# The first unit's rows asked for before a slot's scatter, and their sums and splits in order of use

## The chip, the cores and the metric

One core of a Trainium2 chip runs the whole program. The metric is the device time of one execution in microseconds (us); the median of several runs is compared. TensorE (PE) multiplies matrices, VectorE (DVE) and ScalarE (ACT) work on tiles elementwise, GpSimd (POOL) copies and issues indirect transfers, SyncE (SP) issues most of the other transfers.

## What is computed

```python
attn_out = attention(q, k, v, mem_k, mem_v)     # 4 x 8 heads, 768 tokens, chunks of 32 with a local window
x = attn_out as (3072 tokens, 512)
# routed part: each token goes to one of 8 experts
for e in range(8):
    h = np.maximum(x[mask] @ w1[e], 0.0)        # 512 -> 1024
    out[mask] = gate_w[mask, None] * (h @ w2[e])  # 1024 -> 512
# dense part, on the routed part's output
h = x @ w_in                                    # 512 -> 2048
r = np.maximum(h, 0.0)
return ((r * r) @ w_out).astype(np.float32)     # 2048 -> 512
```

## The kernel before, in words

The program has three parts that run one after the other with some overlap: attention, the routed part, the dense part. Every float32 product is made of three matmuls, on a high and a low part of each operand (`split`, lines 105 and 108: ScalarE casts the high part, VectorE subtracts it from the source).

**The routed part** works through 28 slots of 128 tokens (`s`, up to `NA` = 28; a further three, `NA` to `NS`, stand under a condition at line 1662 and are run only where the number of slots in use asks for them). For each slot: the tokens' rows are gathered (`gather`, POOL), transposed and split (`xtr`), multiplied by the expert's first weights in two halves (`mm1 a`, `mm1 b`, tiles `wh1a`, `wl1a` and so on, PSUM `hps`), passed through ScalarE (`ha`, `hb`), transposed and split (`htr`, tiles `tr`, `hThb`, ...), and multiplied by the second weights (`mm2 a`, `mm2 b`, PSUM `yps`). `finish` (line 1156) scales the result on ScalarE into `ysb`, and POOL scatters it by an indirect transfer (line 1157) to `y_d` in HBM, where the rows stand in the order of the tokens. The weights' high and low tiles are made anew (`renew`, line 998) only where the next slot has another expert; SP then also loads the following expert's raw weights (`r1a` ... `r2b`, line 1015).

**The dense part** (`Ffn`) takes the rows of `y_d` in three units of 1024 tokens. `load_y(u, r)` (line 1266) asks on SP for four tiles of 128 rows, for r = 0 and r = 1; `ytr` (line 1277) transposes them into the four PSUM banks X, Y, Z and W; `ycw` is a list of twelve steps that forms seven operands from the four banks, sums and differences first (`tu`, `tv`, lines 1291 and 1306), then for each a split into `yc` and `yl` (`put`). The first product is a seven-product scheme: `product` (line 1336) is called in the order of operands 1, 6, 5, 7 and then 2, 3, 4 (`FIRST`, `SECOND`), 42 matmuls in all for one step `d`. The second product (`second`, lines 1357 to 1359, PSUM `acc`) follows one step behind.

**How the two meet.** `run` is a generator: `prep` for the first unit's rows, then eight steps `d` and `rest` for each unit. Each `yield` ends a chunk. In the slot loop `ffn_step` is called four times a slot, and in the last slots each call draws one chunk from it:

```python
            if s < NA - 3 or (s == NA - 3 and n < 2):
                return
            n = 1
            while n and pending[0] != "acc":
```

So chunks are drawn from the last call of slot 25 on. After the slot loop a loop over the remaining chunks runs the dense part and, after every second one, `conv.step()`. `conv` (`Convert`) turns w_in and w_out from 64-bit to 32-bit numbers in 64 pieces: an ACT-issued load `rw`, a ScalarE step (line 182), four VectorE operations (lines 190 to 199) and the split. The last 16 pieces, of w_out, are left for the dense part.

The engines execute their instructions in the order in which this code issues them, and tiles of one tag share a buffer: an instruction waits until the buffer's earlier users are done. `y_d` is one tensor for all scatters: a read waits for the scatters issued before it, and a scatter for the reads issued before it.

Of the kernel before, what the change touches and what calls it, by code (L numbers as in the profile page):

```python
# [21 lines left out]
def kernel(  # L22
# [31 lines left out]
    NA = NT + E // 2  # L54
# [48 lines left out]
    def split(hi, lo, src, eng=nc.vector, cp=None):  # L103
        if cp is None:
            nc.scalar.copy(out=hi, in_=src)  # L105
        else:
            cp.tensor_copy(out=hi, in_=src)
        eng.tensor_tensor(out=lo, in0=src, in1=hi.bitcast(F32), op=ALU.subtract)  # L108
# [1054 lines left out]
    class Ffn:  # L1163
# [118 lines left out]
        def ycw(self, r):  # L1282
            b11, b12, b21, b22 = (self.b[h, t] for h in range(2) for t in range(2))
            tmp = {}

            def tmp_tile(n, tag):
                tmp[n] = self.big.tile([P, 512], F32, name="t" + tag, tag=tag)
                return tmp[n]

            def sub(o, a, b):  # L1290
                nc.vector.tensor_tensor(out=o, in0=a, in1=b, op=ALU.subtract)

            def put(i, src):
                def f():
                    if r == 0:
                        pool, tag = self.low[i]
                        self.yc[i] = (
                            self.big.tile([P, 2, 512], F32R, name="yc", tag=f"yc{i}"),
                            pool.tile([P, 2, 512], F32R, name="yl", tag=tag),
                        )  # L1300
                    hi, lo = (z[:, :, r * 256:(r + 1) * 256] for z in self.yc[i])
                    split(hi, lo, (tmp[src] if isinstance(src, str) else src).rearrange("p (k c) -> p k c", k=2))
                return f

            return [
                lambda: nc.scalar.copy(out=tmp_tile("t1", "u2"), in_=b12),
                lambda: sub(tmp_tile("t3", "v"), b22, tmp["t1"]),
                lambda: sub(tmp["t1"], tmp["t1"], b11),
                put(1, b11), put(7, "t3"), put(5, "t1"),
                lambda: sub(tmp_tile("t2", "v"), b22, tmp["t1"]),  # L1310
                put(2, b21), put(6, "t2"),
                lambda: sub(tmp_tile("t4", "u2"), b21, tmp["t2"]),
                put(3, b22), put(4, "t4"),
            ]

        def prep(self):
            wr = [(wres["1a"], f"w{x}1a{i}") for i in range(2) for x in "hl"]
            self.low = dict(zip((1, 7, 5, 2, 6, 3, 4), [(self.big, "yl1"), (self.big, "yl2")] + wr + [(wres["1b"], "wl1b1")]))
            self.load_y(0, 0)
            self.load_y(0, 1)  # L1320
            yield "load"
            for r in range(2):
                self.ytr(0, r)
                ops = self.ycw(r)
                yield "x"
                for n in (4, 4, 4):
                    for _ in range(n):
                        ops.pop(0)()
                    yield "x"
# [164 lines left out]
    with tc.manual_schedule():  # L1494
# [14 lines left out]
        wres, res = {}, {}  # L1509
# [90 lines left out]
        def load_wout(idx):  # L1600
            r0 = (idx - STORED.start) * P
            t = wout_tile(idx)
            nc.sync.dma_start(out=t.bitcast(F32).rearrange("p a f -> p (a f)"), in_=wo_d[r0:r0 + P, :])
# [14 lines left out]
        def ffn_step(n):  # L1618
            quarter[0] += 1
            if quarter[0] % 2 and quarter[0] % 16 != 1:  # L1620
                conv.drain(2)
            elif conv.n - conv.LAST < EARLY:
                conv.step(0)
            if s < NA - 3 or (s == NA - 3 and n < 2):
                return
            n = 1
            while n and pending[0] != "acc":
                pending[0] = next(chunks)
                n -= 1

        pending = [None]
        for s in range(KE, NA):
            if s + 1 < NA:
                moe.mm1(s + 1, "a")
            else:
                conv.until(EARLY)
                conv.flush()
                if ffn.out:
                    ffn.out.pop()()
                for idx in range(5):  # L1640
                    load_wout(idx)
            moe.htr(s, "b")
            ffn_step(1)
            moe.mm2(s, "a")
            if s == NA - 1:
                for idx in range(5, 8):
                    load_wout(idx)
            if s + 1 < NA:
                moe.htr(s + 1, "a")
            ffn_step(1)  # L1650
            if s + 2 < NA:
                moe.xtr(s + 2)
            if s + 1 < NA:
                moe.mm1(s + 1, "b")
            ffn_step(1)
            if s + 3 < NA:
                moe.gather(s + 3)
            moe.mm2(s, "b")
            ffn_step(2)
# [8 lines left out]
                    moe.htr(s, ab)  # L1668
                    moe.mm2(s, ab)
        for k, _ in enumerate(chunks):  # L1670
            if k % 2:
                conv.step()


# [45 lines left out]
```

## Time and profile before

| what | value |
|---|---|
| median of 3 runs | 1007.53 us (1005.34 to 1008.9) |
| the profiled execution | 1008.31 us |
| its span, first to last instruction | 1006.6 us |
| TensorE busy | 956.9 us, 95% |
| DVE busy | 622.1 us, 62% |
| ACT busy | 397.3 us, 39% |
| mean granted TensorE clock | 0.983 of full |

The span is what the trace covers; the execution's own time is 1.7 us longer. All positions below are us from the span's start. Matmuls overlap: a matmul row is longer (0.39 us) than the step to the next one (0.23 us). The same holds, by less, for the rows of ScalarE and VectorE.

### The profile page before, as it was taken

How to read it: one execution, taken by the hardware profiler on the slowest of the kernel's cores; microseconds unless marked ns; L12 is line 12 of the kernel's file. 1: busy time of each engine (PE TensorE's matmuls, PEld its weight loads, DVE VectorE, ACT ScalarE, POOL GpSimd, SP SyncE). 2: the span in 40 equal slices, each digit the busy share in tenths (PEclk: the TensorE clock that was granted, in tenths of full speed). 3: DMA queues.
4: the chain of work that ended last, by engine and by line, in shares of the span. 5: the costliest groups of instructions: out<-in, count | busy, mean ns of one | idle time of the engine just before them, and what ended most of it. 6: DMA issues, size and time to landing. Idle time of an engine off the chain costs nothing. (4 is left out here: it accounts for less than half of the span.)

```text
span 1006.6 us, 17170 instructions
## 1 busy us (share of the span) xinstructions
PE 956.9 (95%) x5982; PEld 778.7 (77%) x5982; DVE 622.1 (62%) x1259; ACT 397.3 (39%) x731; POOL 162.6 (16%) x197
## 2 busy tenths in 40 slices
PE   6889798999999999997799999999999999999997
PEld 5667577888887888886587888878888888888886
DVE  7778795747767686882899454554454554544522
ACT  8656533536555565763533112431111342111221
POOL 8765212111111111210000001010000101000011
PEclk9999799999999999997799999999999999999999
DMA  9993626644948496984465245014443303234011
GB/s 327 362 405 132 236 65 218 208 138 153 328 140 312 170 312 241 332 312 159 175 224 172 91 131 204 1 49 139 147 167 126 126 1 126 93 117 146 1 42 42
DMA packets 62496, 172.94 MB, mean 172 GB/s; under 512 B 7092, under 2 KB 7220, under 8 KB 62400
## 3 DMA queue, kind: packets, MB, share of 16 engines
q1 hardware_dynamic: 43392, 122.45, 34.6%
q0 software_dynamic: 8640, 28.32, 7.9%
q10 hardware_dynamic: 10368, 20.98, 6.0%
q8 instruction: 49, 0.80, 0.3%
q14 instruction: 47, 0.39, 0.1%
HBM read 213.66 MB, written 38.80 MB: 251 GB/s over the span
## 5 line engine op out<-in xcount | busy, mean ns | idle before, releaser
L1357 PE MATMUL acc<-wo,g 128*128 128x512 f32 x384 | 150.9, 393 | 0.2
L1359 PE MATMUL acc<-wo,g 128*128 128x512 f32 x384 | 150.6, 392 | 0.0
L1358 PE MATMUL acc<-wo,g 128*128 128x512 f32 x384 | 149.9, 390 | 0.0
L1382 POOL DMA_INDIRECT out_dram<-osb,oid x24 | 23.6, 983 | 485.5 <-ACT osb L1378 355.6
L1359 PEld LDWEIGHTS acc<-wo,g 128*128 128x128 f32 x384 | 72.1, 188 | 16.9 <-DVE g L108 1.3
L1357 PEld LDWEIGHTS acc<-wo,g 128*128 128x128 f32 x384 | 72.1, 188 | 16.5 <-ACT g L105 1.5
L1402 DVE SCALAR_TENSOR_TENSOR cf<-cf 128x512 f32<-128x512 f32 x54 | 37.1, 692 | 76.8 <-ACT cf L1425 75.9
L1358 PEld LDWEIGHTS acc<-wo,g 128*128 128x128 f32 x384 | 72.2, 188 | 15.5
L1157 POOL DMA_INDIRECT y_d<-ysb,sidx x28 | 33.2, 1186 | 285.5 <-ACT ysb L1156 207.7
L105 ACT CAST g<-cf 128x512 fp32r<-128x512 f32 x54 | 33.5, 621 | 105.7 <-PE acc L1359 74.6
L1425 ACT COPY cf<-zX 128x512 f32<-128x512 f32 x24 | 14.0, 585 | 147.3 <-PE zX L1336 147.3
L1336 PE MATMUL zX<-yc,ww 128*128 128x512 f32 x192 | 68.3, 397 | 2.5 <-PEq L1662 2.5
L1336 PE MATMUL zW<-yc,ww 128*128 128x512 f32 x192 | 67.9, 394 | 0.9 <-DVE cf L1418 0.9
L108 DVE TENSOR_TENSOR g<-gk,g 128x512 fp32r<-128x512 f32 x42 | 29.1, 693 | 63.9 <-ACT g L105 63.3
L1336 PE MATMUL zY<-yc,ww 128*128 128x512 f32 x192 | 68.3, 397 | 0.0
L108 DVE TENSOR_TENSOR g<-cf,g 128x512 fp32r<-128x512 f32 x54 | 37.4, 692 | 31.9 <-ACT g L105 31.2
L105 ACT CAST g<-gk 128x512 fp32r<-128x512 f32 x42 | 26.1, 623 | 73.9 <-PE acc L1359 73.9
L135 POOL COPY kw<-kt 64x672 f32<-64x672 f32 x62 | 51.4, 829 | 10.2 <-PE sp L277 7.6
L1108 PE MATMUL yps<-wh2a,hTha 128*128 128x512 f32 x112 | 47.6, 425 | 0.0
L108 DVE TENSOR_TENSOR hTlb<-tr,hThb 128x512 fp32r<-128x512 f32 x28 | 19.3, 690 | 43.1 <-ACT hThb L105 42.6
L1109 PE MATMUL yps<-wl2a,hTha 128*128 128x512 f32 x112 | 45.5, 406 | 0.0
L1110 PE MATMUL yps<-wh2a,hTla 128*128 128x512 f32 x112 | 45.4, 405 | 0.0
(327 smaller groups left out, 2278.0 us busy)
## 6 DMA issues: line engine op xcount, KB each, us to landing
ww<-wi_d SPq DMA_DIRECT2D x77, 512.0 KB
r1a<-in_moe_w_dram SPq DMA_DIRECT2D x54, 512.0 KB
r1b<-in_moe_w_dram SPq DMA_DIRECT2D x54, 512.0 KB
r2a<-in_moe_w_dram SPq DMA_DIRECT2D x52, 512.0 KB
r2b<-in_moe_w_dram SPq DMA_DIRECT2D x52, 512.0 KB
wi_d<-ww SPq DMA_DIRECT2D x28, 512.0 KB
vb<-in_v_dram SPq DMA_DIRECT2D x32, 390.0 KB
rw<-in_moe_w_in_dram ACTq DMA_DIRECT2D x32, 256.0 KB
```

Source lines behind the costliest of these rows:

```text
L105: nc.scalar.copy(out=hi, in_=src)
L108: eng.tensor_tensor(out=lo, in0=src, in1=hi.bitcast(F32), op=ALU.subtract)
L135: (nc.vector if eng == "v" else nc.gpsimd).tensor_copy(out=out, in_=in_)
L1108: nc.tensor.matmul(out=out_ps, lhsT=ah, rhs=wh, start=first, stop=False)
L1109: nc.tensor.matmul(out=out_ps, lhsT=ah, rhs=wl, start=False, stop=False)
L1110: nc.tensor.matmul(out=out_ps, lhsT=al, rhs=wh, start=False, stop=last)
L1157: nc.gpsimd.indirect_dma_start(out=y_d[:, :], out_offset=bass.IndirectOffsetOnAxis(ap=sidx[:, s:s + 1], axis=0), in_=y, in_offset=None, bo ...
L1336: nc.tensor.matmul(out=z, lhsT=w[:, d % 2, wx, kt], rhs=y[yx][:, kt, :], start=start and (kt, x) == (0, 0), stop=(kt, x) == (1, 2), skip_g ...
L1357: nc.tensor.matmul(out=self.acc[j], lhsT=g[:, 0, c], rhs=wt[:, 0], start=first, stop=False)
L1358: nc.tensor.matmul(out=self.acc[j], lhsT=g[:, 0, c], rhs=wt[:, 1], start=False, stop=False)
L1359: nc.tensor.matmul(out=self.acc[j], lhsT=g[:, 1, c], rhs=wt[:, 0], start=False, stop=last)
L1402: nc.vector.scalar_tensor_tensor(out=o, in0=x, scalar=0.0, in1=x, op0=ALU.max, op1=mul)
```

## The change

- `prep` issues `load_y(0, 0)` in a chunk of its own, and `load_y(0, 1)` in the next. `ffn_step` draws from the third call of slot 25 on (that call now passes 2), so that the first four tiles are asked for before `mm2 b` and the scatter of slot 25, and the other four after it.
- In `ycw` the sums are formed in another order (the third one, `t3`, from `t2`), and operand 6 is split before 5 and 7 later, in the order of the products; the buffers of the low parts are dealt out in that order (`low`).
- The chunks of `prep` hold other numbers of steps: 3, 4, 5, 0 for r = 0 (with the transposes in the first), and 0, 4, 4, 4 for r = 1.
- `conv.step()` runs after every third chunk of the dense part, not after every second.

```diff
             return [
                 lambda: nc.scalar.copy(out=tmp_tile("t1", "u2"), in_=b12),
-                lambda: sub(tmp_tile("t3", "v"), b22, tmp["t1"]),
                 lambda: sub(tmp["t1"], tmp["t1"], b11),
-                put(1, b11), put(7, "t3"), put(5, "t1"),
                 lambda: sub(tmp_tile("t2", "v"), b22, tmp["t1"]),
-                put(2, b21), put(6, "t2"),
+                put(1, b11), put(6, "t2"), put(5, "t1"),
+                lambda: sub(tmp_tile("t3", "u2"), tmp["t2"], b11),
+                put(2, b21), put(7, "t3"),
                 lambda: sub(tmp_tile("t4", "u2"), b21, tmp["t2"]),
                 put(3, b22), put(4, "t4"),
             ]
...
-            self.low = dict(zip((1, 7, 5, 2, 6, 3, 4), [(self.big, "yl1"), (self.big, "yl2")] + wr + [(wres["1b"], "wl1b1")]))
+            self.low = dict(zip((1, 6, 5, 2, 7, 3, 4), [(self.big, "yl1"), (self.big, "yl2")] + wr + [(wres["1b"], "wl1b1")]))
             self.load_y(0, 0)
+            yield "load"
             self.load_y(0, 1)
             yield "load"
-            for r in range(2):
+            for r, counts in enumerate(((3, 4, 5, 0), (0, 4, 4, 4))):
                 self.ytr(0, r)
                 ops = self.ycw(r)
-                yield "x"
-                for n in (4, 4, 4):
+                for n in counts:
                     for _ in range(n):
                         ops.pop(0)()
                     yield "x"
...
-            if s < NA - 3 or (s == NA - 3 and n < 2):
+            if s < NA - 3 + (n < 2):
                 return
...
             if s + 1 < NA:
                 moe.mm1(s + 1, "b")
-            ffn_step(1)
+            ffn_step(2)
             if s + 3 < NA:
                 moe.gather(s + 3)
             moe.mm2(s, "b")
...
         for k, _ in enumerate(chunks):
-            if k % 2:
+            if k % 3 == 1:
                 conv.step()
```

On SP, where the first unit's rows are asked for behind the last loads of `r2a`, the eight loads stand in the same order as before; the first five read before (DMASW are the semaphores of POOL's transfers, DMAHW those of SP's and ACT's):

```order
L1266 DMA ys<-y_d 128x512 [waits DMASW1_49]
L1266 DMA ys<-y_d 128x512
L1266 DMA ys<-y_d 128x512 [waits DMAHW6_49]
L1266 DMA ys<-y_d 128x512 [waits DMAHW7_49]
L1266 DMA ys<-y_d 128x512 [waits DMAHW0_49,DVE_49,Activation_49]
```

and now:

```order
L1266 DMA ys<-y_d 128x512 [waits DMASW0_49]
L1266 DMA ys<-y_d 128x512
L1266 DMA ys<-y_d 128x512 [waits DMAHW6_49]
L1266 DMA ys<-y_d 128x512 [waits DMAHW7_49]
L1266 DMA ys<-y_d 128x512 [waits DMASW1_49,DMAHW0_49,DVE_49,Activation_49]
```

The first load waits for an earlier transfer of POOL's, and the wait for `DMASW1` has moved to the fifth. POOL's scatter of slot 25 now waits for four of these loads, and that of slot 26 for the other four.

On DVE, at the turn from slot 26 to slot 27, around the renewal of `wl2a`, the rows before were (`tu` and `tv` are the sums, `zX` to `zW` the banks):

```order
L108 TENSOR_TENSOR wl2a_2402<-r2a_2217,wh2a_2401 128x1024
L998 UNCONDITIONAL_BRANCH x2
L108 TENSOR_TENSOR yl<-tv,yc 128x2x256
L108 TENSOR_TENSOR yl<-tu_7170,yc 128x2x256
L1291 TENSOR_TENSOR tv<-zW,tu_7170 128x512
L108 TENSOR_TENSOR yl<-zZ,yc 128x2x256
L108 TENSOR_TENSOR yl<-tv,yc 128x2x256
L1291 TENSOR_TENSOR tu_7234<-zZ,tv 128x512
```

and now:

```order
L108 TENSOR_TENSOR wl2a_2402<-r2a_2217,wh2a_2401 128x1024
L998 UNCONDITIONAL_BRANCH x2
L108 TENSOR_TENSOR yl<-zZ,yc 128x2x256
L108 TENSOR_TENSOR yl<-tu_7187,yc 128x2x256
L1291 TENSOR_TENSOR tu_7217<-zZ,tv 128x512
```

Behind `wl2a` stand two operations, no longer five, before the sum that reads bank Z last; the three others stand ahead of `wl2a`.

On ACT, at the same place, the rows before were:

```order
L105 CAST hTha<-tr 128x512 [waits DVE_49,PE_49]
L1306 COPY tu_7170<-zY 128x512
L105 CAST yc<-zX 128x2x256 [waits DVE_49]
L998 COMPARE_AND_BRANCH
L105 CAST wh2a_2399<-r2a_2216 128x1024 [waits DMAHW2_49,Activation_49]
L105 CAST wh2a_2401<-r2a_2217 128x1024 [waits DMAHW3_49,Activation_49]
L998 UNCONDITIONAL_BRANCH
L998 UNCONDITIONAL_BRANCH [waits Activation_49]
L1125 ACTIVATE hb<-hps 128x512 [waits PE_49,Activation_49]
```

and now:

```order
L1306 COPY tu_7148<-zY 128x512 [waits PE_49]
L105 CAST hTha<-tr 128x512 [waits DVE_49,PE_49]
L105 CAST yc<-zX 128x2x256 [waits DVE_49]
L105 CAST yc<-tv 128x2x256 [waits DVE_49]
L105 CAST yc<-tu_7148 128x2x256
L998 COMPARE_AND_BRANCH
L105 CAST wh2a_2399<-r2a_2216 128x1024 [waits DMAHW2_49,Activation_49]
L105 CAST wh2a_2401<-r2a_2217 128x1024 [waits DMAHW3_49,Activation_49]
L998 UNCONDITIONAL_BRANCH
L998 UNCONDITIONAL_BRANCH [waits Activation_49]
L1125 ACTIVATE hb<-hps 128x512 [waits PE_49,Activation_49]
```

The copy of bank Y goes ahead of `hTha`, and two casts of `yc` have moved ahead of the `wh2a` casts and of `hb`, for which the next transposes wait.

## Rows read from the trace of the kernel before

**Rows 1.** The page, section 2: granted TensorE clock in 40 slices, tenths of full.

```profile
PEclk9999799999999999997799999999999999999999
```

**Rows 2.** TensorE's waits, 440 to 620 us: us in total, times, longest.

```profile
PE zX L1277 <- DMA ys<-y_d: 3.9, 2, 3.6
PE zZ L1277 <- DVE tu L1291: 3.5, 1, 3.5
PE zX L1336 <- PEq L1662: 2.5, 1, 2.5
PE zY L1277 <- DMA ys<-y_d: 2.4, 2, 2.1
PE zW L1336 <- DVE cf L1418: 0.9, 2, 0.5
```

**Rows 3.** TensorE's timeline: start, duration, instruction, count [idle before and its releaser].

```profile
458.18 0.60 PE L1132 MATMUL tr<-ident,hb 128*128 128x128 f32 x4
...
467.85 0.76 PE L1108 MATMUL yps<-wh2a,hTha 128*128 128x512 f32 x1
...
472.39 0.60 PE L1132 MATMUL tr<-ident,ha 128*128 128x128 f32 x4
...
483.56 0.72 PE L1277 MATMUL zZ<-identr,ys 128*128 128x128 f32 x4 [3.55 <-DVE tu L1291]
...
484.67 0.76 PE L1108 MATMUL yps<-wh2a,hTha 128*128 128x512 f32 x1
...
489.31 0.40 PE L1108 MATMUL yps<-wh2b,hThb 128*128 128x512 f32 x1
...
491.84 0.39 PE L1110 MATMUL yps<-wh2b,hTlb 128*128 128x512 f32 x1
494.73 0.47 PE L1336 MATMUL zX<-yc,ww 128*128 128x512 f32 x1 [2.50 <-PEq L1662]
```

**Rows 4.** SP's timeline, 430 to 510 us: issues of transfers.

```profile
452.99 0.63 SPq L1015 DMA_DIRECT2D r2a<-in_moe_w_dram  x2
459.57 3.67 SPq L1266 DMA_DIRECT2D ys<-y_d  x8
```

**Rows 5.** POOL's timeline: the scatters of slots 24 and 25.

```profile
444.41 1.00 POOL L1157 DMA_INDIRECT y_d<-ysb,sidx  x1 [8.99 <-ACT ysb L1156]
456.62 1.16 POOL L1157 DMA_INDIRECT y_d<-ysb,sidx  x1 [11.21 <-ACTq L998]
```

**Rows 6.** Line 1157, 400 to 500 us: landing of the scatters.

```profile
DMA to landing us min/median/max: 2.8/3.8/8.1
```

**Rows 7.** Windows: us, busy time of each engine (instructions), clock, DMA share, GB/s.

```profile
455.00:456.00 1.00, 1.00 (x6) 0.84 (x5) 1.00 (x2) 0.83 (x2) 0.00 (x0) 1.00 0.08 31
463.00:464.00 1.00, 0.62 (x3) 0.44 (x3) 0.00 (x0) 0.00 (x0) 0.00 (x0) 0.50 0.94 307
```

**Rows 8.** ScalarE's timeline, 452 to 506 us.

```profile
473.03 0.59 ACT L105 CAST hTha<-tr 128x512 fp32r<-128x512 f32 x1 [13.52 <-PE tr L1132]
...
476.18 2.00 ACT L105 CAST wh2a<-r2a 128x1024 fp32r<-128x1024 f32 x2
...
484.44 1.99 ACT L105 CAST wh2b<-r2b 128x1024 fp32r<-128x1024 f32 x2
```

**Rows 9.** VectorE's timeline, 452 to 506 us.

```profile
482.73 0.68 DVE L1291 TENSOR_TENSOR tu<-zZ,tv 128x512 f32<-128x512 f32 x1
...
485.53 2.36 DVE L108 TENSOR_TENSOR wl2b<-r2b,wh2b 128x1024 fp32r<-128x1024 f32 x2
```

**Rows 10.** Line 1662: count, duration in ns, start, on TensorE's sequencer.

```profile
L1662 PEldq COMPARE_BRANCH  x1: 5872/5872/5872, 488.5 to 488.5; - x1
```

**Rows 11.** DMA queues, 492 to 492.5 us: packets, MB, share of 16 engines.

```profile
q1 hardware_dynamic: 43, 0.17, 84.8%
q8 instruction: 1, 0.02, 11.7%
```

**Rows 12.** Windows in the dense part; columns as in rows 7.

```profile
530.00:540.00 10.00, 9.59 (x42) 7.51 (x41) 9.20 (x23) 3.23 (x8) 0.00 (x0) 1.00 0.27 87
540.00:550.00 10.00, 9.47 (x42) 7.43 (x41) 9.67 (x25) 3.23 (x8) 0.00 (x0) 1.00 0.78 262
```

## Prediction

> **What bounds the kernel now.** I read the page's row of granted clock first: it is full but for the start and two neighbouring slices, the 19th and 20th of 40, where it falls to 0.7 [rows 1]. These are 453 to 503 us, the passage from the last slots to the dense part. The list of TensorE's waits over 440 to 620 us says why: 12.3 us of idle time in three places and 0.9 us in a fourth [rows 2]. TensorE is busy without a break around them, so what is saved there on the path into the dense part is saved at the end. The places, in TensorE's timeline [rows 3]:
>
> First, after slot 26's `htr` (458.18 + 0.60 = 458.78) the next slot matmul starts only at 467.85. Between stand 16 transposes of y rows that wait for their loads. SP asked for the rows at 459.57, although it was through with its load before at 453.62 [rows 4]: it waited for slot 25's scatter, begun at 456.62 [rows 5].
>
> Second, at 483.56 bank Z's transposes of the second half wait 3.6 us for DVE's `tu<-zZ,tv`, which ends at 483.41 [rows 2, 3, 9].
>
> Third, after slot 27's last matmul (491.84) the first product starts at 494.73, held by the jump over the spare slots, line 1662 [rows 3]. The jump's row begins at 488.5, 0.6 us after DVE ended `wl2b` (485.53 + 2.36 = 487.89), and lasts 5.87 us [rows 9, 10]. TensorE's sequencer gets there only when the waits of slot 27's last matmuls are met, and `wl2b` meets the last of them.
>
> Each gap is followed by matmuls at the lower of the clock's two levels (1.2 GHz; the granted clock is 0.50 at 463 to 464 [rows 7]): the 12 of slot 26's `mm2 a` take 4.54 us (467.85 to 472.39), those of slot 27's 4.64 (484.67 to 489.31), while `mm2 b` at the full clock has 11 steps in 2.53 us, 0.23 each or 2.8 for 12 [rows 3].
>
> **Part 1, four tiles asked for before slot 25's scatter.** The first ask now waits for the scatter of slot 24, begun at 444.41 [rows 5]; landing took at most 8.1 us in this stretch [rows 6], so it is done by 452.5 and SP asks at 453.6, 5.9 us earlier. By 455 to 456 us the transfers have run dry, 31 GB/s [rows 7], so the four, 1.05 MB at about 300 GB/s [rows 7], take 3.5 us and some 1 us of start: landed by about 458.3. TensorE wants them at 458.8. From below the price is no stall at all. From above it is the pace of before, where eight were asked for together and mm2 followed at most 8.3 us after the ask (467.85 - 459.57): that gives 461.9 instead of 460.1. I take a loss of 0.3, nearer the first, since half as many bytes are queued.
>
> So the 16 transposes start at 458.6. Eight take 1.11 us at the lower clock (483.56 to 484.67) [rows 3], so 16 take about 1.5 at the full one; `mm2 a` starts at 460.1, 7.8 us earlier. At the full clock it takes 2.8 instead of 4.5: slot 27's `htr a` comes at 462.9, **9.5 us earlier** than 472.39.
>
> The wait is not gone but moved: slot 25's scatter now waits for the four reads (458.3 instead of 456.6). It lands some 3 us later (456.62 to the ask at 459.57 [rows 4, 5]) at 461.3, and the other four tiles, asked for then, are there by 466. The second set of transposes wants them at 469.2. Behind them on SP stand only the w_out reads, which wait for slot 27's `mm1 b` anyway (466.1).
>
> **Part 2, the order of sums and splits.** ScalarE's chain from `hTha` (473.03; 0.6 us after `htr a`, now 463.5) has two more casts, 1 us, ahead of the `wh2a` casts and `hb`. Against that, the first cast no longer waits for its subtraction: before, the casts began 3.15 us after `hTha` [rows 8], now about 2.05 (four casts of 0.5): 465.6 to 467.6. `hb` ends at 468.1; TensorE wants it at 468.8. So these cost nothing, with 0.7 us to spare. DVE then ends `wl2a` at 469.5. To `tu<-zZ,tv` it is now the third operation behind, not the sixth; they step by 0.6, each row being 0.68 long [rows 9], so it ends at 471.4. TensorE, ready for bank Z at 470.3, waits some 1.2 us where it waited 3.6. Three ScalarE operations later (`yc`, `ysb`, `hThb`) `wh2b` starts at 473.0 against 484.44, and `wl2b`, 1.09 behind and 2.36 long [rows 8, 9], ends at 476.4 against 487.9: **11.5 us earlier**. TensorE's last slot matmul starts at about 477.9 against 491.84, 13.9 earlier.
>
> **Part 3, the jump.** Its time decides which of the two shifts counts. Counted from the jump's row, 5.87 us, the first product starts 6.84 us behind `wl2b`: 483.3, a gain of 11.5. Counted from the last matmul's start, 2.89 us, it starts at 480.8, a gain of 13.9. A block of instructions (0.02 MB) came within 492.0 to 492.5 while the data queue held the engines at 84.8% [rows 11]. That traffic, three w_out reads behind `mm2 a`, lies about 1.5 us earlier against the jump now. I take 482.2, between the two: **a gain of 12.5**.
> The Trainium skill's page "Runtime: NRT & Kernel Launch", section "Instruction fetch mechanics", says that a taken branch to a target outside the window forces a fetch before execution goes on. By that rule the time counts from the jump and the gain is the lower, 11.5; the trace agrees that the row starts before the matmuls run out, and shows nothing of the window.
>
> The idle time before the product grows from 2.5 to about 4 us, so the low stretch behind it will be nearer that after the second gap (12 matmuls in 4.64 instead of 2.8, 1.9 lost) than today's shorter one: a loss of 1.0.
>
> **Part 4, w_out pieces on every third chunk instead of every second.** DVE is busy 9.2 and 9.67 of 10 us at 530 to 550 us, and TensorE loses 0.41 and 0.53 there [rows 12], the wait for `cf L1418` of rows 2. With a third fewer pieces per chunk that goes: a gain of 0.9. The 16 pieces left then end at chunk 46 (one at k = 1, 4, ... 46), the first of them is needed at chunk 52, so nothing is late. From below: 0. The same reordering in the later units lies beside a TensorE that is never idle there: nothing.
>
> **Sum**: 12.5 - 0.3 - 1.0 + 0.9 = 12.1 us. The profiled execution took 1008.31 us (span 1006.6), 0.8 over the median of the three runs, 1007.53; 1007.53 - 12.1 = **995.4 us**.
>
> **The rivals.** (a) The first rows still come late: 461.9 instead of 460.1, and the clock falls again for one `mm2` (1.7 us). That is 1.5 + 1.7 = 3.2 us less gained: 998.6. For it speaks that tiles of eight came apart by microseconds (waits of 3.9 and 2.4 us on two banks [rows 2]); against it the empty queue at 455 [rows 7].
> (b) The second rows come late, since their ask now stands behind a scatter that stands behind reads. With the slowest of all, reads landed at 460.5 (461.9 less the transposes), 8.1 for the scatter [rows 6] and 6.9 for the loads (8.3 less the transposes), they land at 475.5, 6.3 us after they are wanted: 5.8 gained, 1001.7.
> (c) Slower: TensorE's clock stays at the lower level from the first remaining gap through to the dense part. The place is 458 to 500 us, the price 0.2 us for each matmul; 60 slot matmuls and 42 of the first products cost 20 us, 15 more than the 5 lost there today, against some 12 from the gaps (8.5 of the first two, 2.5 of the jump, then hidden) and part 4: 3 slower, 1010.5. It decides from some 85 slow matmuls on. Against it: after each of today's gaps, longer ones, the clock came back; `mm2 b` behind the second one runs at 0.23 a step from 489.31 [rows 3].
> (d) The change does not do what it says: the ask still waits for slot 25's scatter. SP's listed wait is another semaphore now, so hardly; then some 3 us from parts 2 and 4 are left, 1004.5.
>
> **How the numbers follow.** A measurement can tell about 0.3%, 3 us, from no change. Forecast 0.74, (a) 0.13, (b) 0.05, (c) 0.04, (d) 0.04. The forecast's own range is 992.5 to 998: the two ends of part 3, 0 to 0.9 in part 4, and a run's spread. Widened to (a) and the edge of (b), and by a microsecond below for a jump that finds a free queue: 991 to 1001. Faster by over 0.3%: forecast, (a), (b) and half of (d), 0.92 when a little is kept for what I do not see. Within 0.3%: 0.04. Slower: 0.04.
>
> **What would show it.** Ask of the first four rows at about 453.6, no wait of over 1 us on the first transposes; slot 25's scatter some 1.7 us later; bank Z's wait down to about 1.2; `wl2b` ending at about 476.4; the jump's row beginning 0.6 later and lasting 4 to 6 us, which becomes the largest gap left; no wait of zW on `cf L1418`. It is wrong if the first four rows land after 460, if `hb` holds `htr b` (part 2's 0.7 us gone), or if the jump lasts longer than 5.9.

## The result, and the profile after

The changed kernel takes 997.24 us (median of 6 runs, 994.94 to 998.83) against 1007.36 us (6 runs, 1004.34 to 1008.90) of the kernel before on the same chip: a ratio of 0.9902, 95% interval 0.9883 to 0.9922. It is 10.1 us faster; 12.1 were forecast, and the time lies inside the range. The profiled execution took 997.39 us, its span is 995.7 us.

The granted clock, on the page of the kernel after: where two slices fell to 0.7 before [rows 1], one falls to 0.8.

```profile
PEclk9999799999999999999899999999999999999999
```

TensorE's waits at 440 to 620 us, as in [rows 2]; columns: us in total, times, longest.

```profile
PE zX L1336 <- PEq L1662: 3.9, 1, 3.9
PE zZ L1277 <- DVE tu L1291: 1.7, 1, 1.7
PE zY L1277 <- DMA ys<-y_d: 0.3, 1, 0.3
```

13.2 us in four places have become 5.9 us. The two waits for the first unit's rows are down from 6.3 to 0.3, bank Z's from 3.5 to 1.7, the one on `cf` is gone, and the jump's has grown from 2.5 to 3.9. Here is TensorE's timeline of the kernel after, which answers to [rows 3]; columns: start, duration, instruction, count, idle before and its releaser.

```profile
457.59 0.60 PE L1132 MATMUL tr<-ident,hb 128*128 128x128 f32 x4
...
458.83 0.45 PE L1277 MATMUL zY<-identr,ys 128*128 128x128 f32 x3 [0.26 <-DMA ys<-y_d]
...
459.81 0.46 PE L1108 MATMUL yps<-wh2a,hTha 128*128 128x512 f32 x1
...
462.64 0.60 PE L1132 MATMUL tr<-ident,ha 128*128 128x128 f32 x4
...
468.56 0.60 PE L1132 MATMUL tr<-ident,hb 128*128 128x128 f32 x4
...
471.44 0.51 PE L1277 MATMUL zZ<-identr,ys 128*128 128x128 f32 x4 [1.65 <-DVE tu L1291]
...
479.25 0.39 PE L1110 MATMUL yps<-wh2b,hTlb 128*128 128x512 f32 x1
483.57 0.77 PE L1336 MATMUL zX<-yc,ww 128*128 128x512 f32 x1 [3.94 <-PEq L1662]
...
488.83 0.50 PE L1336 MATMUL zZ<-yc,ww 128*128 128x512 f32 x1
```

Slot 26's `htr` stands 0.59 us earlier than before (457.59 against 458.18), though the change touches nothing ahead of slot 25. In the fourteen executions profiled here it lies anywhere from 457.6 to 465.6, so what comes ahead of it differs from run to run. Below, a position is therefore counted from slot 26's `htr` of the same execution where two kernels are compared: from it to the first product ("head") 36.55 us before (494.73 - 458.18) and 25.98 now (483.57 - 457.59), 10.57 less; from the first product to the span's end ("tail") 511.87 before (1006.6 - 494.73) and 512.13 now, 0.26 more. Together 10.3 us less, near the 10.1 of the runs. These sums hold to about a microsecond: two executions with the same code up to the first product have heads of 36.55 and 35.84 us (before, and the conversions alone of experiment 3), and the changed kernel has 25.98 and, in a second execution (experiment 7), 24.81, with a tail of 512.03.

The engines that feed TensorE there, in the same kernel: SP's asks and POOL's scatter of slot 25 (as [rows 4, 5]), ScalarE's `hb`, VectorE's last sum on bank Z and `wl2b` (as [rows 8, 9]).

```profile
453.08 11.12 SPq L1266 DMA_DIRECT2D ys<-y_d  x8
```

```profile
459.56 0.98 POOL L1157 DMA_INDIRECT y_d<-ysb,sidx  x1 [14.74 <-ACT hThb L105]
```

```profile
467.18 0.60 ACT L1125 ACTIVATE hb<-hps 128x512 f32<-128x512 f32 x1
```

```profile
470.61 0.69 DVE L1291 TENSOR_TENSOR tu<-zZ,tv 128x512 f32<-128x512 f32 x1
...
474.00 2.36 DVE L108 TENSOR_TENSOR wl2b<-r2b,wh2b 128x1024 fp32r<-128x1024 f32 x2 [0.26 <-ACT wh2b L105]
```

The first four tiles are asked for at 453.08, ahead of the scatter, and the eight asks are now spread over 11.12 us, because the last four wait for the scatter. `hb` ends at 467.78, 0.78 us ahead of the transposes that read it (468.56). And the jump (as [rows 10]; duration in ns, start) is longer than before:

```profile
L1662 PEldq COMPARE_BRANCH  x1: 6246/6246/6246, 477.0 to 477.0; - x1
```

In the dense part the windows that lost 0.41 and 0.53 us on TensorE [rows 12] are now full; columns as there.

```profile
530.00:540.00 10.00, 10.00 (x45) 8.10 (x44) 7.51 (x20) 2.60 (x6) 0.00 (x0) 1.00 0.90 316
540.00:550.00 10.00, 10.00 (x45) 8.16 (x44) 9.16 (x20) 2.60 (x6) 0.00 (x0) 1.00 0.27 106
```

### The profile page after: what moved, and what is told of

It is laid out like the page before. It is cut to its first block, busy times and chain, and to the rows that moved or that the text cites. A ratio compares the mean times of both kernels' runs of the same rounds, so it can differ in the third digit from the quotient of the medians.

```text
span 995.7 us, 17168 instructions
## 1 busy us (share of the span) xinstructions
PE 954.9 (96%) x5982; PEld 777.0 (78%) x5982; DVE 623.1 (63%) x1259; ACT 397.2 (40%) x731; POOL 162.2 (16%) x197
## 4 chain that ended last, share of the span: by engine, by line
issue 36%; PE 12%; POOL 2%; POOLq 0%; DVE 0%; ACT 0%; ACTq 0%
PE zX L1336 2%; PE zY L1336 2%; PE zW L1336 2%; POOL out_dram L1382 2%; PE acc L1359 1%; PE acc L1357 1%; PE acc L1358 1%; PE zZ L1336 1%; POOLq L1716 0%; POOLq L1382 0%; DVE g L108 0%; ACT g L105 0%; ACTq L105 0%
## 5 line engine op out<-in xcount | busy, mean ns | idle before, releaser
L1336 PEld LDWEIGHTS zX<-yc,ww 128*128 128x128 f32 x192 | 36.5, 190 | 12.6 <-ACTq L1662 4.3
```

Source lines behind the costliest of these rows:

```text
L1336: nc.tensor.matmul(out=z, lhsT=w[:, d % 2, wx, kt], rhs=y[yx][:, kt, :], start=start and (kt, x) == (0, 0), stop=(kt, x) == (1, 2), skip_g ...
```

## The experiments

What had to be told apart: which part of the change brings the gain, and whether the jump's length is a fixed price, a matter of TensorE's last slot matmuls, or one of the transfers beside it.

### 1 to 4: the parts of the change by themselves

**Early rows alone**: the change without the new order of sums, the new counts and the conversions on every third chunk. Against the kernel before:

```diff
             self.load_y(0, 0)
+            yield "load"
             self.load_y(0, 1)
...
-            if s < NA - 3 or (s == NA - 3 and n < 2):
+            if s < NA - 3 + (n < 2):
...
-            ffn_step(1)
+            ffn_step(2)
```

> The first four tiles asked for ahead, everything else as before. Theory (the shift is that of the end of wl2b, and the early ask carries most of it): the first transposes wait under 1 us as in the changed kernel, slot 27's htr a comes some 9.5 us earlier than before, bank Z again waits about 3.6 us, wl2b ends 15.5 us behind htr a as before, so at about 478 to 478.5, some 2 us later than in the changed kernel; zW waits 0.9 us on cf L1418 again. About 9 us under the kernel before, 998 to 999. Rival (the order of sums and splits carries most): the gain of the early ask is eaten by a longer wait for bank Z, of 6 us or more, and the time stays within 4 us of the kernel before.

Measured: 999.86 us (998.41 to 1001.02, 4 runs), ratio 0.9927 [0.9905, 0.9949]. TensorE's waits in this kernel, same stretch (its lines lie one higher from 1320 on):

```profile
PE zZ L1277 <- DVE tu L1291: 3.5, 1, 3.5
PE zX L1337 <- PEq L1663: 3.0, 1, 3.0
PE zW L1337 <- DVE cf L1419: 1.0, 2, 0.5
PE zY L1277 <- DMA ys<-y_d: 0.3, 1, 0.3
```

The rows' waits have gone, bank Z's stays as it was. Head 27.24 us, 9.3 less than before; by the runs 8.1 us less than the kernel before on the same chip (1007.95 us, 13 runs), where about 9 was expected. Asking early is by far the larger part of the gain.

**Order alone**: the kernel before with the new `ycw`, `low` and counts, the rows asked for together as before. Of its diff, which is that part of the change:

```diff
-            for r in range(2):
+            for r, counts in enumerate(((3, 4, 5, 0), (0, 4, 4, 4))):
```

> The new order of sums and splits and the new chunks, all eight tiles asked for behind slot 25's scatter as before, w_out pieces on every second chunk as before. Theory: the first gap stays (about 9.3 us between htr of slot 26 and the next slot matmul), bank Z waits 1 to 2 us instead of 3.6, wl2b ends about 2 us earlier than before: 1005 to 1006. Rival (order carries most): over 5 us under the kernel before.

Measured: 1007.49 us (1005.7 to 1010.8, 10 runs), ratio 1.0001 [0.9982, 1.0019]. Its waits:

```profile
PE zX L1277 <- DMA ys<-y_d: 3.8, 2, 3.5
PE zX L1335 <- PEq L1661: 3.2, 1, 3.2
PE zY L1277 <- DMA ys<-y_d: 1.7, 2, 1.5
PE zZ L1277 <- DVE tu L1291: 1.6, 1, 1.6
```

Bank Z's wait falls from 3.5 to 1.6 as in the full change, and the head is 34.13, 2.4 less. Head and tail together are 2.1 us less in this one execution, but the runs show no gain (0 within 1.9 us), and the 1005 to 1006 us that were expected were missed. So the order does in the trace what it says, and its worth in time is not shown by itself.

**Conversions on every third chunk alone**, and **the full change with them on every second**:

```diff
-            if k % 2:
+            if k % 3 == 1:
```

> The kernel before with w_out pieces on every third chunk. Theory: the wait of zW on cf L1418 (0.9 us) is gone, nothing else moves; a time that cannot be told from the kernel before. Rival (pieces come late): a wait of acc on wo or wf of over 1 us around the fifth step.

> The changed kernel with w_out pieces on every second chunk again. Theory: the waits of zW on cf L1418 come back with about 0.9 us, the chain up to the jump stays where it is in the changed kernel (wl2b ends near 476.4). Rival: the waits do not come back, since they had another cause, and part 4 gives nothing.

Measured: 1007.2 and 998.9 us, one run each, with which a microsecond can't be told. The traces show it: in the first no wait on `cf` is left and the tail is 510.58 us against 511.87; in the second a wait is back, once and not twice, 0.5 us and not 0.9, and the tail is 513.21 against 512.13 with the full change. `wl2b` ends 18.69 us behind slot 26's `htr` there, with the full change 18.77: the chain ahead of the jump has not moved, as expected.

```profile
PE zW L1336 <- DVE cf L1418: 0.5, 1, 0.5
```

So part 4 is worth 1.1 to 1.3 us by single executions.

### 5: what the jump waits for

The three reads of w_out that SP is asked for behind slot 27's `mm2 a` moved behind the conditional block, all else as in the change:

```diff
-            if s == NA - 1:
-                for idx in range(5, 8):
-                    load_wout(idx)
...
+        for idx in range(5, 8):
+            load_wout(idx)
         for k, _ in enumerate(chunks):
```

> The changed kernel with the last three w_out reads issued behind the jump over the spare slots, not ahead of it. Theory (the jump's block of instructions queues behind those 1.6 MB): the jump lasts about 4 us instead of 6.2, and the gap before the first product shrinks from 3.9 to about 2; some 2 us faster in the profile. Rival (the jump's time is its own, whatever the transfers): it lasts 5.7 to 6.3 us and nothing changes.

Measured: 997.41 us, one run, in an execution whose slot 26 came 4.0 us later than that of the changed kernel. The jump's row (line 1659 here) and the DMA queues from its start to the block of instructions:

```profile
L1659 PEldq COMPARE_BRANCH  x1: 3366/3366/3366, 480.8 to 480.8; - x1
```

```profile
q8 instruction: 1, 0.02, 5.6%
q0 software_dynamic: 10, 0.01, 2.3%
q10 hardware_dynamic: 2, 0.00, 0.1%
```

In the changed kernel the queues from the jump's start (477.0) to the block at 480.8 to 480.9 look like this, and in the tenth of a microsecond of the block itself like that:

```profile
q1 hardware_dynamic: 319, 1.18, 93.7%
```

```profile
q8 instruction: 1, 0.02, 62.1%
```

The same block of 0.02 MB came 1.0 us behind the jump's row where the transfers stood still, and 3.8 us behind it where they held the engines at 93.7%. The gap before the first product was 2.3 us, near the 2 expected. One execution could be chance, so the same kernel was run again, more often:

> The kernel with the three w_out reads behind the conditional block and nothing ahead of it, a second profile and timed. Theory (the jump is an instruction block that queues behind the data reads, then a fixed 2.7 us): the block is there within 1.5 us of the jump's row, where it took 3.1 to 3.8 with the reads ahead; the first product starts 2.7 us behind the block; time 2 to 4 us under the changed kernel, 993 to 995, ratio to the kernel before 0.984 to 0.987. Rival (the first short block was chance, its length varies by itself): block 3 us or more after the jump's row, gap of 3 to 4.5 us, time 997, ratio 0.988 to 0.990.

Measured: 994.68 us (992.83 to 995.84, 6 runs), ratio 0.9870 [0.9844, 0.9895]. Time and block came as expected. The block came at 477.8 to 477.9, again 1.0 us behind the row; the jump's row, and the first product:

```profile
L1659 PEldq COMPARE_BRANCH  x1: 3512/3512/3512, 476.9 to 476.9; - x1
```

```profile
480.70 0.77 PE L1336 MATMUL zX<-yc,ww 128*128 128x512 f32 x1 [2.51 <-PEq L1659]
```

All executions in which nothing was issued between the slots and the jump, put side by side (us, to within 0.1; the block is put in the middle of the tenth of a microsecond in which q8's one packet is found):

| kernel | jump's row | block, behind the row | first product, behind the block |
|---|---|---|---|
| before | 488.5 | 3.5 | 2.7 |
| order alone | 486.5 | 3.2 | 2.7 |
| conversions alone | 488.6 | 3.5 | 2.8 |
| early rows alone | 479.4 | 3.2 | 2.8 |
| changed kernel | 477.0 | 3.8 | 2.7 |
| the same, profiled again | 479.3 | 3.1 | 2.7 |
| changed, every second chunk | 479.4 | 1.8 | 2.7 |
| changed, reads behind | 480.8 | 1.0 | 2.7 |
| the same, profiled again | 476.9 | 1.0 | 2.8 |

The second interval is 2.7 to 2.8 us everywhere; all the difference lies in the first, which is shortest in the two executions without the reads. The rival, that the length varies by itself, has the 1.8 of one kernel for it, but the reads differ there too: the queue q1 falls below half of the engines' time for good 3.2 us behind the row, in the six other executions with the reads 3.8 to 4.6 us (in windows of 0.2 us), and in all seven the block comes before that. A third execution with still queues is the one with four chunks ahead in experiment 7, where the reads are asked for ahead of the jump but are through when it begins, at 485.5: its block came 1.0 us behind the row.
The Trainium skill's page "DMA: Bandwidth & Descriptors", section "Queues, rings and completion order", says that an engine works through a whole packet of several descriptors of one queue before it turns to the next queue, and gives 9 to 17 as typical. As an estimate: 319 pieces of q1 in 3.8 us on 16 engines are 0.19 us each, and the 2.1 to 2.8 us by which the block came later behind the reads are 11 to 15 of them; in the execution with 1.8 us it is 0.8 us, or 4. The traces agree in size; where a packet ends none of them shows.

### 6: hiding the jump, or doing without it

Two, or four, chunks of the first product issued ahead of the conditional block (line 1660), so that TensorE has matmuls in its queue when the sequencer jumps:

```diff
+        for _ in range(4):
+            next(chunks)
         cnt = nc.values_load(cnt_i[0:1, 0:1], min_val=0, max_val=NS)
```

> The changed kernel with two chunks (the products of operands 1 and 6, 12 matmuls) issued ahead of the jump. Theory (the jump counts from the last wait of the matmuls ahead of it, and runs beside those that are queued): it begins near 479.7, once the low part of operand 6 is there, 2.8 us of products run beside it, and the third product starts about 486 instead of 488.8: 1 to 3 us faster than the changed kernel. Rival (the jump waits until the matmuls ahead of it are through): the gap only moves behind the products, unchanged at about 4 us, and the time stays.

> The same with four chunks (operands 1, 6, 5 and 7, 24 matmuls). Theory: the jump begins near 482, when operand 7's low part is there; 5.5 us of products lie ahead, so the gap is about 3 us; 1 to 3 us faster than the changed kernel, near that with two. Rival: as with two, the gap moves and stays at about 4.

And the change without the conditional block, which leaves the three spare slots out, and with them their prefetch and the jump:

```diff
-        cnt = nc.values_load(cnt_i[0:1, 0:1], min_val=0, max_val=NS)
-        moe.prefetch()
-        with tc.If(cnt > NA):
-            for s in range(NA, NS):
...
         for k, _ in enumerate(chunks):
```

> The changed kernel without the conditional block of the three spare slots, which these inputs don't use; left out are those slots and the jump. Theory: the gap of 3.9 us goes and with it the low clock behind it (2.4 us): 5 to 6.5 us faster than the changed kernel, 991 to 992. Rival (DVE's splits of the second half come next): the first products wait for yl instead, and less than 3 us are gained.

Measured: with two chunks 996.94 us (994.53 to 999.33, 4 runs), ratio 0.9877 [0.9847, 0.9907]; with four 995.04 (992.94 to 1000.11, 4 runs), 0.9883 [0.9848, 0.9919]; without the block 993.68 (991.78 to 999.48, 5 runs), 0.9845 [0.9821, 0.9870]. With two chunks a jump's gap of 2.2 us is left in front of bank Z, and the product of bank Z starts 27.73 us behind slot 26's `htr`, 3.5 us sooner than in the changed kernel (31.24): the theory's way, though the runs are only 0.3 us below the changed kernel's 997.24. With four no wait for the jump is left, where a gap of 3 us was expected:

```profile
L1664 PEldq COMPARE_BRANCH  x1: 1030/1030/1030, 484.8 to 484.8; - x1
```

No block of instructions came within this row; one came 1.9 us before it. In the second execution with four chunks (experiment 7) the row lasted 3.40 us, and TensorE had no wait for it either. With two chunks the block came 0.9 us behind the row and the next product 3.5 us behind the block, not 2.7: the table's second span is that of the kernels with no product issued ahead of the jump.

With four chunks TensorE starts the first product at 481.35, 23.02 us behind slot 26's `htr`, and does the 12 matmuls of banks X and Y in 2.84 us, at the full clock, where the changed kernel took 5.26 (483.57 to 488.83). Without the block the waits are:

```profile
PE zZ L1277 <- DVE tu L1291: 1.7, 1, 1.7
PE zX L1336 <- DVE tu L1291: 1.1, 1, 1.1
```

So the next thing that is late is VectorE: the first product overwrites bank X, which the sum `tu<-tv,zX` reads last. Without a jump the first product comes 22.71 us behind `htr`, 3.3 less than in the changed kernel, and its 12 matmuls take 2.84 us here too, 2.4 less: these 5.7 us are all that is to be had from the jump, by one execution of each; against the second execution of the changed kernel (24.81 and 5.25 us) they are 4.5. The runs are 3.6 us apart (993.68 and 997.24), less than the 5 to 6.5 expected.

### 7: the changed kernel and two better ones side by side

The changed kernel once more, the one with four chunks ahead, and one with both edits, four chunks ahead and the reads behind the block.

> The changed kernel as it is, timed beside the two others of this call. Both theories: about 997 us, ratio to the kernel before 0.990; its jump over the spare slots lasts 4 to 6 us in the profile and TensorE idles 3 to 4 us at the first product of the dense part.

> The changed kernel with four chunks of the first product issued ahead of the conditional block. Theory (the jump's gap and the low clock behind it are on the path that sets the end): faster than the changed kernel of this call by 2 to 5 us (3.9 us of gap and 2.4 us of low clock go, about 0.6 us of a new wait for a sum comes), that is 992 to 995. Rival (the gap only moves, and what sets the end lies elsewhere): within 1 us of the changed kernel of this call.

> The same, with the three w_out reads moved behind the conditional block as well. Theory: the jump is hidden already, so the reads in its way cost nothing any more: within 1 us of the kernel with four chunks ahead. Rival (the reads also slow something else there, such as the fetch behind the jump): 1 to 3 us faster than it. If the reads come too late for the second product, a wait on wo shows in TensorE's list and it is slower.

Measured, 6 runs each: 997.57 us (994.67 to 999.42), ratio 0.9883 [0.9858, 0.9908]; 995.63 (994.09 to 998.12), 0.9874 [0.9849, 0.9898]; 995.62 (993.61 to 997.71), 0.9868 [0.9844, 0.9892]. In this second execution the changed kernel's jump lasted 5.5 us, and TensorE idled 4.5 us at the first product, more than the 3 to 4 expected. Its rows of slot 26's `htr`, the first product, `wl2b` and the jump:

```profile
460.36 0.60 PE L1132 MATMUL tr<-ident,hb 128*128 128x128 f32 x4
...
485.17 0.77 PE L1336 MATMUL zX<-yc,ww 128*128 128x512 f32 x1 [4.51 <-PEq L1662]
```

```profile
476.33 2.36 DVE L108 TENSOR_TENSOR wl2b<-r2b,wh2b 128x1024 fp32r<-128x1024 f32 x2 [0.25 <-ACT wh2b L105]
```

```profile
L1662 PEldq COMPARE_BRANCH  x1: 5506/5506/5506, 479.3 to 479.3; - x1
```

The waits with four chunks ahead, and the first product:

```profile
PE zX L1336 <- DVE tu L1291: 2.3, 1, 2.3
PE zZ L1277 <- DVE tu L1291: 1.7, 1, 1.7
```

```profile
482.21 0.77 PE L1336 MATMUL zX<-yc,ww 128*128 128x512 f32 x1 [2.27 <-DVE tu L1291]
```

The jump's wait is gone, but here VectorE's sum ended at 482.06 and holds bank X for 2.3 us, after which TensorE again runs low (12 matmuls in 4.41 us). In experiment 6 the same wait was 0.6 us: there the 12 matmuls of slot 27's `mm2 a` took 4.46 us and TensorE came to the product later, here 2.86. Head and tail come to 534.1 us against 536.8 of the changed kernel beside it. The medians are 1.9 us lower, where 2 to 5 were expected; the ratios' intervals overlap, so that these versions beat the changed kernel is likely and not shown by the runs. The reads moved as well change nothing more (995.62 against 995.63), as the theory had it. The same goes for the reads behind the block alone (994.68): all of these versions beat the kernel before, and none is shown to beat the changed kernel. Only without the jump at all is the interval (0.9821 to 0.9870) clear of the one of the changed kernel's first measurement (0.9883 to 0.9922), and it overlaps that of the second (0.9858 to 0.9908).

## Why the prediction was right, and where it was off

**What bounds the kernel** held: the head, with the three named places, became 10.57 us shorter, and the tail changed by 0.26.

**Part 1** held. The ask was forecast at 453.6 and came at 453.08; the first tiles cost 0.26 us of waiting where 0.3 was taken; slot 25's scatter came 2.9 us later, not 1.7 (459.56 against 456.62; 3.5 later counted from `htr`), and was hidden, as the spread of SP's asks was. Counted from slot 26's `htr`, slot 27's `htr a` came 9.16 us earlier (14.21 before, 5.05 now): the 9.5 less the 0.3. Alone, this part took 9.3 us off the head. Rival (a) and rival (b) are out: no row load was waited for longer than 0.3 us.

**Part 2** held in the trace, to within half a microsecond. The 0.7 us that `hb` had to spare are 0.78. Bank Z waited 1.65 us, not 1.2, and `wl2b` came 10.94 us earlier (29.71 us behind `htr` before, 18.77 now; 18.33 in the second execution, 11.38 earlier) where 11.5 less 0.3 was forecast. What this part gives by itself no run shows.

**Part 3 is the term that was off, by its size.** Between the two ways to count, from the jump's row (a gain of 11.5) and from the last slot matmul (13.9), the prediction took 12.5. It is counted from the row. From the last slot matmul's start to the first product it took 2.89 us before and 4.32 now, from the end of `wl2b` 6.84 and 7.21: the first grew by what was saved, the second hardly moved. The second execution of the changed kernel (experiment 7) says the same, with 4.90 and 6.48: its last slot matmul stood 1.75 us nearer to `htr` than in the first (19.91 against 21.66), its first product only 1.17, 0.47 by the row and 0.7 by the block.
The head fell by 10.57 us in the one execution and by 11.74 in the other, where 12.2 (12.5 - 0.3) was forecast. In both, 1.0 us of the miss is the splitting of the difference. The jump, counted from `wl2b`, was 0.4 longer than before in the one and 0.4 shorter in the other, so that part belongs to the execution and not to the change.
The 13.9 had a flaw of its own, which the prediction did not see: it takes the clock to be full for slot 27's `mm2 a`, behind bank Z's wait. The wait was the same in both executions (1.65 and 1.66 us), yet the 12 matmuls took 4.15 us in the first, most of it at a granted clock of 0.50, and 2.84 in the second, at 1.00. So the last slot matmul came 12.0 us earlier in the one and 13.75 in the other, and the first product did not follow it.
The Trainium skill's page "Runtime: NRT & Kernel Launch", section "Instruction fetch mechanics", whose rule gave 11.5, is borne out by the traces: the product came 2.7 to 2.8 us behind a block of instructions in the nine executions of the table, and with still queues that block was there 1.0 us behind the jump's row. What the block holds no trace shows.
The reason given for taking less than the row's price was that the w_out reads lie earlier against the jump. That points at the right cause, and experiment 5 shows its worth (3.8 us down to 1.0), but the reads did not clear the jump: they held the engines at 93.7% up to the block. The text named a jump of over 5.9 us as a sign that it is wrong; the two executions have 6.25 and 5.51 us, so by itself this sign decides nothing.

**The low clock behind the jump** was forecast at 1.0 us more and was 0.85: the 12 matmuls of banks X and Y took 5.26 us (5.25 in the second execution) against 4.41. Rival (c) is out: from 488.83 on the matmuls of banks Z and W step by 0.23 us again, as they did behind the gaps of the kernel before.

**Part 4** was put at 0.9 and is 1.1 to 1.3 us in single executions. With 0.85 lost to the clock the tail should have become shorter by some 0.3; it is 0.26 longer. Most of these 0.6 us lies in a term that the prediction put at nothing, the reordering in the later units. From the second unit's first transposes to the last matmul the three executions with the old order of sums took 378.71 to 378.77 us, the eleven with the new one 379.10 to 379.18: 0.4 us more, spread thinly over the steps and with no wait of TensorE's beside it. Why is not shown, and it is less than runs can tell. Rival (d) is out with the ask at 453.08.

In all, 12.2 - 0.1 = 12.1 was forecast, 10.57 - 0.26 = 10.3 came in the first execution and 11.74 - 0.16 = 11.6 in the second; by the runs 10.1 and, beside the second, 11.2. With part 3 by the row alone the sum would have been 11.1.

## What to carry to other kernels

Before a block under a condition that is jumped over, give TensorE independent matmuls to work on (12 left a gap of 2.2 us here, 24 none), or keep large transfers out of the microseconds in which the jump happens; that either pays is likely by these runs and not shown. Otherwise count its price from the moment at which the sequencer reaches it, not from the end of the work ahead of it. A read that is held back by a write to the same tensor is best asked for ahead of that write where the rows it needs are ready, and it pays to see first that the write can bear the wait. Where two prices differ by what they are counted from, look for the event that both share (here the instruction block) before settling in the middle.

## What the hardware showed that was not expected

- A jump on TensorE's sequencer is made of two spans: until one block of 0.02 MB arrives on the instruction queue, 1.0 us with still data queues and 1.8 to 3.8 us behind reads, and then 2.7 to 2.8 us to the first matmul, the same in nine executions. With 12 matmuls issued ahead the second span was 3.5 us, and in one execution with 24 the row was over in 1.0 us with no block in it.
- Behind the same wait for bank Z (1.65 to 1.66 us) the clock fell in some executions and not in others: in eleven with the new order the 12 matmuls of slot 27's `mm2 a` took 2.84 to 2.89 us at a granted clock of 1.00 in six, and 4.03 to 4.46 us, with the clock at 0.50 for most of it, in five.
- The same code up to slot 25 brought slot 26's `htr` at 457.6 to 465.6 us in fourteen executions; without a common point in both traces a shift of a few microseconds can't be read from one execution of each.
